# Delta-rule recurrences feeding an MLP mixer: a stretch of the hand-written issue order is rewritten

## Chip, cores and metric

One Trainium2 chip, one of its cores. The metric is device microseconds (us) of one execution of the whole program; several executions are timed and their median is given. One further execution is recorded by the hardware profiler; its times are used for everything that is said about single instructions.

## What is computed

Two blocks follow each other. The first is a delta-rule attention over 4 batch elements, 8 heads, 768 positions and head size 48; the second is an MLP-mixer over its output (768 positions x 384 channels for each batch element). Everything is float32.

```python
k_n = k / (norm(k) + 1e-06)
state = zeros((B, H, D, D))
for t in range(S):
    y[:, :, t] = q[:, :, t] @ state
    v_old = state applied to k_n[:, :, t]
    state += beta[t] * outer(k_n[:, :, t], v[:, :, t] - v_old)
x = y.transpose(0, 2, 1, 3).reshape(B, S, H * D)          # 4 x 768 x 384
xt = x.transpose(0, 2, 1)
h = maximum(xt @ w_tok1, 0) @ w_tok2                      # mixes 768 positions through 256
u = x + h.transpose(0, 2, 1)
out = u + maximum(u @ w_ch1, 0) @ w_ch2                   # mixes 384 channels through 1536
```

## The kernel before

The sequence is cut into chunks of 64 positions, so that one chunk of all 8 heads is handled by small matmuls instead of 64 single steps. Two chunks form a unit of 128 positions. There are 24 units (6 for each batch element) and 48 chunks (12 for each). Units 0 to 5 belong to the first batch element, 6 to 11 to the second, 12 to 17 to the third.

The kernel is written as many small jobs, each a Python generator. Each `next()` on a job issues a handful of instructions, a step, and a long text, `order`, says which job takes its next step when. `p11*4` is four steps of job `p11`. Nothing reorders the result: on each engine, and on the DMA queue that SP issues, instructions run in exactly the order in which the steps stand, each engine at its own pace and held up only by its own waits. This text is therefore a schedule for six queues at once. A step is written here as job and count: r9.5 is the fifth step of r9. The jobs, with their lines:

- `k`u loads keys and queries of unit u (lines 360 to 413); `v`u loads values (413) and scales them on POOL (423, 426).
- `p`u prepares a unit: norms, a masked scale on POOL (511), and turned keys and queries, by PE transposes (499, 519) with ACT copies (503, 524) in units below 12 and by DVE transposes (369) later.
- `c`u and `d`u are the products of keys with keys and queries (PE, 452) and their masking (DVE, 455), for the two chunks of a unit.
- `t`u, `i`round, `f`u invert the triangular 32 x 32 blocks of a unit. Rounds 0 to 6 take several units each; round 2 is units 6 to 9, round 3 is units 10 to 13. A round is 30 pairs of DVE operations, each pair dependent on the one before (676 and 681: i2.2 to i2.31 in round 2), between a DMA in (670) and a DMA out (700); `t` (623) and `f` (648) carry the blocks to and from device memory.
- `h`u and `j`u join inverted blocks into 64 x 64 ones: a DVE transpose (750), 32 x 32 matmuls (780, 783, 788, 821, 829), and ACT copies out of PSUM (799, 802, 806, 755, 834). A wide join has its products at eight places in two PSUM banks.
- `r`t is one chunk's recurrence, a chain through three engines: r.1 to r.4 the product of keys and state (PE, 857, tile `p_k`), r.5 `rest` = that less the values (DVE, 864), r.6 `p_y` and `p_w` (PE, 877 and 881; it needs the unit joined, that is, the last copies of `j`), r.7 the copy `w_t` (ACT, 887), r.8 `p_s` and `p_y` (PE, 895 and 896), r.9 the new state (DVE, 904), r.10 the output (ACT, 909), which also frees the PSUM of `p_y`. The first chunk of a batch element has no r.1 to r.4 of this kind and one step less after them. The tiles `p_k`, `p_y`, `p_w`, `p_s` share two PSUM buffers.
- `m`b is the mixer of batch element b: m.1 to m.6 the first product (PE, 1055), one step for each unit, which needs both chunks of that unit; then the second product (1068), transposes (1078), the channel product (1135 for the first batch element, 1027 later) and the last product (1157), with adds and combinations on DVE (1072, 1086, 1109).
- `w`n loads and rounds a piece of the weights: DMA (271), two ACT operations (277, 278), one DVE operation (280), one POOL operation (284), for some also DVE differences (299); `s` builds sums of weights on DVE (966, 968).
- `z` is one 128 x 128 by 128 x 512 matmul on zeros (225), `Y` four 64 x 64 by 64 x 128 matmuls on zeros (235). They compute nothing that is used. Each is two rows in the profile for each matmul, as is every float32 matmul here.

The DMA queue, the ACT queue and the DVE queue each carry recurrence steps and preparation steps mixed. The part of the text that the change rewrites is at lines 1249 to 1275.

Of the kernel before, what the change touches and what calls it, by code (L numbers as in the profile page):

```python
# [23 lines left out]
def kernel(  # L24
# [1232 lines left out]
    f9*2 w32 f9 j9 f9 r13*2 f8 m0 r13 t10 r13 w31 w32 c11 w32*2 d11*2 c11 v8 c11*3  # L1257
    d11 r14*2 d11*2 r14*3 v8*2 w31*2 r13 w31 k13*5 w30 p12*3 m0*3 r14 c12 d12 c12
    d12 c12 d12 r14 d12 k13*2 r14*3 m0 k13 d12 w30*3 c12*2 v8*2 p13*3 r15*3 k13*4
    r15 t11*3 t12*2 r15 m0*2 r15*2 p13*2 w29 p13 w25 p13 m0*5 r15*2 w33*2 p11 c13*2  # L1260
    d13*2 c13*2 d13 r16*2 k14 c13 d13*2 w33*3 k14*2 r16*2 m0*2 w23 w33 w31*2 w23
# [13 lines left out]
    s*2 m0 i4 m0*2 i4*2 m0 i4*5 v12*4 m0*2 j13 i4*2 m0 i4 r23 j13 m0 r24 k18*3  # L1275
    r24*3 j13 v13*2 r24 i4 r24*2 p18 i4 p18 m0 i4 p18 m0*2 i4*2 m0 r25*3 p18 r25
    p18*2 r25 m1*3 k18*2 v14 i4 v14 r24 i4*7 k19 m1*3 i4 r25 i4*2 k19*3 v13 k19*2
    v14*2 m1 r25 v13 i4*4 k19 m1 p18 m1 k19 r25*2 p18 m1*2 r26 v13 d18 r26*4 j13
    r25 m1*3 r26*2 c18*2 m1*2 r26*2 k19*4 p19*2 d18*3 c18*2 d18 f14*2 v14 r27*2
    f14*2 r27 p19*2 r27 p19 j14 r27 m1*4 s m1*2 f15*3 m1*2 c18 r26 m1*2 r27*2 j14  # L1280
    j15 j14 r27 f16 m1*3 j15*2 r27 r28*2 k20 p19*2 f16 r27 r28*2 k20*2 f16 j16 m1*4
    r28*3 f15 m1*2 s k20*2 s p19 r28 k20*3 d19 c19 k20 d19 p20 c19 t18 k20 d19*2
    p20 c19 v15 r28 p20 r29 k20*2 m1 p20 r28 c19 r29*3 v15*3 f17*2 r29 m1 p20 k21
    m1*2 c19 k21 r29*2 m1*2 d19 k21 m1*2 p20 m1*2 p20 m1*4 r29*3 m1*2 j16*2 r30
    k21*3 v16 k21*2 v15 k21 r30*4 v16 k21*2 m1 k21 m1*2 c20 r30 d20 c20*3 p21*2 c20
    r30*2 p20 d20 r30 d20*2 p21*2 d20 r31*2 r30 r31*2 t18 r31*3 p21*3 m1*2 r31*2
    c21 d21 c21 d21 c21 d21 v16 m1 v16 c21 v16 r32 d21 r32 d21 m1 t18*2 m1 r32 r31
    t19*2 r32*2 f17 m1 f17 m1*4 t19*2 c21 m1*5 p21 m1*2 f16 t20*3 j17*2 t20 t21*4
# [56 lines left out]
```

## Time and profile before

| what | value |
|---|---|
| time, median of 3 | 639.58 us (638.39 to 640.07) |
| the profiled execution's own time | 637.11 us |
| its span, first to last instruction | 635.3 us |
| PE (matmul) busy | 607.5 us, 96% |
| DVE busy | 446.2 us, 70% |
| ACT busy | 268.5 us, 42% |
| POOL busy | 108.2 us, 17% |
| mean granted TensorE clock | 0.981 |

A busy PE is not a PE at its peak: matmuls overlap, and a matmul's row is longer than the distance to the next one. In the views of single instructions the columns are start, duration (or the stretch that a merged row covers), engine, source line, operation, output and inputs, and in brackets the engine's idle time before it and what ended it. In the views of stretches, each engine's busy time is followed by its number of instructions, then come the granted clock (1.00 is full), the busy share of the DMA engines and their rate.

### The profile page before, as it was taken

The numbers are of one execution on the slowest core, as the hardware profiler recorded it, in microseconds if no ns is written. First come the engines' busy times: TensorE is split into PE (matmuls) and PEld (weight loads), VectorE is DVE, ScalarE is ACT, GpSimd is POOL, SyncE is SP. The second block draws the span as 40 slices with busy tenths as digits, with TensorE's granted clock in tenths as the row PEclk, the third lists the DMA queues.
The fourth block names the chain that finished last, engine by engine and source line by source line (L and its number), as shares of the span: only waits on it lengthen the run. The fifth ranks groups of instructions, "written<-read, shape, count | busy, mean of one in ns | idle before, by whom it ended". The sixth has DMA issues, their size and how long they took to land.

```text
span 635.3 us, 21547 instructions
## 1 busy us (share of the span) xinstructions
PE 607.5 (96%) x9132; PEld 529.5 (83%) x9132; DVE 446.2 (70%) x1132; ACT 268.5 (42%) x693; POOL 108.2 (17%) x146
## 2 busy tenths in 40 slices
PE   8488898999999999999999999999999999999997
PEld 5367786667888888858999999769999977999997
DVE  4988877977899667987969987785627253373643
ACT  7759785447512342226624433145254230223240
POOL 2338354235310221111110010101010000000000
PEclk9979896999999999999999999999999999999999
DMA  9787566666542445154444033201020000000000
GB/s 201 129 148 166 140 134 162 170 135 157 110 115 74 82 118 110 50 125 77 95 101 103 14 95 47 66 11 37 2 54 2 27 1 0 26 1 26 2 26 26
DMA packets 135776, 50.27 MB, mean 79 GB/s; under 512 B 114656, under 2 KB 130144, under 8 KB 135680
## 3 DMA queue, kind: packets, MB, share of 16 engines
q1 hardware_dynamic: 135680, 48.89, 34.9%
q8 instruction: 72, 1.18, 0.8%
q14 instruction: 24, 0.20, 0.1%
HBM read 39.42 MB, written 9.44 MB: 77 GB/s over the span
## 4 chain that ended last, share of the span: by engine, by line
PE 78%; DVE 7%; ACT 5%; SPq 3%; DMA 3%; issue 2%; POOL 1%; ACTq 0%; POOLq 0%; DVEq 0%
PE p_o L1157 25%; PE p_r L1027 18%; PE p_c L1135 8%; PE p_h L1068 5%; PE p L1055 4%; PE p_s L895 3%; PE p_g L452 3%; PE p_k L857 3%; PE p_y L877 2%; DVE x L681 1%; DVE sub L676 1%; PE p_w L881 1%; SPq L413 1%; PE p_ut L1078 1%; DMA d<-in_moe_w_ch_dram 1%
## 5 line engine op out<-in xcount | busy, mean ns | idle before, releaser
L1157 PE MATMUL p_o<-wc,r 128*128 128x192 f32 x720 | 126.8, 330 | 0.6 <-ACT u_t L1082 0.6
L1157 PEld LDWEIGHTS p_o<-wc,r 128*128 128x128 f32 x720 | 116.6, 190 | 2.9 <-ACT u_t L1082 1.1
L1039 DVE TENSOR_TENSOR r<-r,p_r 128x512 f32<-128x512 f32 x90 | 59.7, 684 | 39.7 <-PE p_r L1027 37.2
L1086 DVE TENSOR_TENSOR xb<-xb,p_o 128x192 f32<-128x192 f32 x84 | 29.3, 350 | 58.7 <-PE p_o L1157 58.4
L1036 ACT COPY r<-p_r 128x512 f32<-128x512 f32 x54 | 31.5, 586 | 89.4 <-PE p_r L1027 88.0
L681 DVE TENSOR_TENSOR x<-x,sub 128x84 f32<-128x84 f32 (+24 forms) x178 | 59.8, 336 | 6.1
L676 DVE TENSOR_TENSOR sub<-x 128x84 f32<-128x84 f32 (+24 forms) x178 | 57.4, 322 | 6.7 <-DMA x<-n_dram 2.3
L1135 PE MATMUL p_c<-u_t,wc 128*128 128x256 f32 x216 | 51.1, 387 | 0.2 <-ACT u_t L1082 0.2
L1157 PE MATMUL p_o<-wc,s 128*128 128x192 f32 x288 | 50.1, 329 | 0.3 <-DVE xb L1086 0.3
L426 POOL TENSOR_TENSOR v_st<-v_st,nrm 128x384 f32<-128x384 f32 x24 | 20.3, 845 | 166.7 <-DMA v_st<-in_v_dram 129.1
L1157 PEld LDWEIGHTS p_o<-wc,s 128*128 128x128 f32 x288 | 46.8, 190 | 1.2 <-DVE xb L1086 0.6
L1135 PEld LDWEIGHTS p_c<-u_t,wc 128*128 128x128 f32 x216 | 39.6, 190 | 6.1 <-ACT u_t L1082 0.4
L1043 ACT ACTIVATE r<-r 128x512 f32<-128x512 f32 x54 | 33.8, 630 | 25.0 <-DVE r L1039 24.6
L452 PE MATMUL p_g<-kq 48*64 48x128 f32 (+1 forms) x704 | 38.6, 283 | 3.0 <-ACT kq L524 2.8
L511 POOL TENSOR_TENSOR mb<-mask_c,cs 128x512 f32<-128x512 f32 x20 | 21.4, 1072 | 108.0 <-DVE cs L489 40.9
L909 ACT ACTIVATE xb<-p_y 64x192 f32<-64x192 f32 x96 | 31.2, 325 | 19.6 <-PE p_y L896 12.1
L1027 PE MATMUL p_r<-u_t,wc 128*128 128x128 f32 x288 | 38.5, 277 | 0.0
L1027 PE MATMUL p_r<-t_d,wc 128*128 128x128 f32 x288 | 37.2, 280 | 0.0
L887 ACT COPY w_t<-p_w 128x192 f32<-128x192 f32 x48 | 15.3, 318 | 50.0 <-PE p_w L881 49.3
L1027 PEld LDWEIGHTS p_r<-u_t,wc 128*128 128x128 f32 x288 | 35.3, 192 | 0.3
L1055 PE MATMUL p<-xb,w 128*128 128x384 f32 x96 | 34.9, 511 | 0.0
L452 PEld LDWEIGHTS p_g<-kq 48*64 48x64 f32 (+1 forms) x704 | 28.9, 137 | 7.1 <-ACT kq L524 3.7
(184 smaller groups left out, 1216.0 us busy)
## 6 DMA issues: line engine op xcount, KB each, us to landing
d<-in_moe_w_ch_dram SPq DMA_DIRECT2D x24, 384.0 KB, 4.2
v_st<-in_v_dram SPq DMA_DIRECT2D x96, 48.0 KB, 2.7
out_dram<-xb SPq DMA_DIRECT2D x23, 192.0 KB, 1.9
kst<-in_k_dram SPq DMA_DIRECT2D x64, 48.0 KB, 2.8
n_dram<-gm SPq DMA_DIRECT2D x72, 32.0 KB, 2.0
pads<-in_k_dram SPq DMA_DIRECT2D x24, 96.0 KB, 3.1
pads<-in_q_dram SPq DMA_DIRECT2D x24, 96.0 KB, 2.5
gm<-w_dram SPq DMA_DIRECT2D x72, 32.0 KB, 2.1
```

The source lines that it names most:

```text
L452: nc.tensor.matmul(p_g[PAR[i ^ cc], p], kqt[f, p, cc, 0], kqt[f, p, cc])
L676: nc.vector.tensor_tensor(out=tmp, in0=y[:, :, 0:s, s : s + 1].to_broadcast([n, k, s, w]), in1=y[:, :, s : s + 1, s + 1 : m].to_broadcast( ...
L681: nc.vector.tensor_tensor(out=y[:, :, 0:s, s + 1 : m], in0=y[:, :, 0:s, s + 1 : m], in1=tmp, op=ALU.add,)
L909: nc.scalar.mul(y[:, :, D * i : D * i + D], p_y[PAR[1 - i]], 1.0 if c else -1.0)
L1027: nc.tensor.matmul(p[:, i], pieces[i // width][:, at : at + 128], f[f"u{n}"], start=first and i == 0, stop=True, skip_group_check=True,)
L1036: nc.scalar.copy(o, p)
L1039: nc.vector.tensor_tensor(out=o, in0=o, in1=p, op=ALU.add if sign > 0 else ALU.subtract)
L1043: nc.scalar.activation(o, o, ACTF.Relu)
L1055: nc.tensor.matmul(p_1[dh], piece_of(w1, c, 0)[:, dh * 128 : (dh + 1) * 128], xb[:, c], start=(c == 0), stop=(c == NCH - 1),)
L1068: nc.tensor.matmul(p_h, piece_of(w2, j, c * 128)[:, c * 128 : (c + 1) * 128], r1[j], start=(j == 0), stop=(j == NDH - 1),)
L1135: nc.tensor.matmul(p_c[:, k], piece_of(wc1, cb, f * 128)[:, f * 128 : (f + 1) * 128], u_t[:, cb], start=(cb == 0), stop=(cb == NCB - 1),)
L1157: nc.tensor.matmul(p, a[:, m], wc2[:, m, j], start=(start and i == 0), stop=(i == NM - 1), skip_group_check=True,)
```

## The change

Only the text `order` changes. The steps up to k11.2 and h5.6, just after r8.9, stand as before, and so do those from the loads of unit 18 and round 4 on (k18, i4, r24), apart from weight sums and one step of f12; between them, over the recurrences r9 to r23, the second and third inversion rounds, the units' preparation and most of the first mixer block, the same steps stand in another order. Jobs take the same steps; only the matmuls on zeros differ in number: two `z` are added and two of three `Y` in the stretch are gone. The functions and the PSUM layout are unchanged, the joins' eight places in two banks among them.

The first lines of the diff, which carry the recurrences r9 to r13:

```diff
-    w29 w27*2 r8*2 w29*3 j4*2 r8 w22*4 t9*4 r8*3 p10 h5*2 k11 h5 j5 Y i2 r9*3 r8
-    r9*2 i2*4 j5 i2*3 r9*2 i2 h5 k12*2 j5 Y r9*2 m0 v6 k11 j5 p9 w4*2 r10*3 i2*2 j5
-    k10 r10 p10*4 w4 v5 i2 v5*3 r9 k11*2 v5 r10*3 i2 w4 i2*3 w15*3 w19*2 i2 w19 m0
-    i2 w12 r10*2 m0*2 r11 r10 p11 k12*4 w19 p11 p10 k12*2 p12 Y i2 w25 r11*3 d10*4
-    r11*2 v7 c10*3 w15 k12 i2*2 w21 i2*4 v6*3 r11*2 i2*3 k11 r11 v7*4 i2*4 c10
-    k12*3 m0*4 c10 m0*2 w25 m0 w12 d10 f6*4 f7*2 p11*2 m0*3 w12 w21 w12 p12 p11*2
-    m0*2 f7 w21*2 j6*2 j7 v6 p12 w25*3 f8*2 w27*2 m0 j6 j7*2 m0 r12*5 f8 f7 j8*2
-    r12 m0 w23*4 j8 r12 t10 r12 t10*2 r13 p10 w23 r13*4 w20*2 p11*3 p12*2 w20*2
...
+    w29 w27*2 r8*2 w29*3 j4*2 r8 w22*4 t9*4 r8*3 p10 h5*2 k11 h5 p9 h5 m0 w4*3 i2
+    j5 i2*3 r9*4 z r8 r9 k11*2 p10*2 i2*4 p10 i2 j5*2 r9*4 m0 r10 k10 p10*2 w21 w4
+    w21 v5*2 i2*2 z i2*2 r10 d10 r10*2 j5 r9 i2 m0 v5 d10 v5*2 w19*2 r10 j5 r10
+    c10*2 i2*3 k12 w19 k12*5 w15*3 k12 w19 r10*3 v7*3 r10 c10*2 r11*2 d10*2 r11 i2
+    r11 m0 r11 w15 r11 k11*2 p11 i2*9 w25 i2*3 v6 r11*2 v6*3 r11 m0*3 k12 v7 k12*2
+    i2 w12*2 i2 m0*2 c10 d10 t10 m0*5 w12*2 t10 p11 w25 p11*4 v6 w25 p12*3 w21 m0*3
+    p10 f6*3 j6*3 w21 w23*2 w25 f7*3 m0 f7 f6 j7*2 m0 f8*3 j7 r12*2 w27*2 f9 r12 j8
+    r12 v7 r12*2 w23*3 w32*2 t10*2 r12*2 k12 w32*2 j8*2 r13*5 Y p12*2 p11*2 w25
...
```

Further on, in the same manner, the third inversion round (i3), the preparation of units 10 to 17 and the recurrences r13 to r23 are dealt differently among the steps of the mixer; four of the weight sums, which stood among r18 to r23, come together after them:

```diff
-    i3 v10*3 m0*7 p15 m0*3 r18*2 m0 f10*4 m0*3 r18 s f12*2 v10 r18 s p14 s m0 r18
...
-    c15*2 r21 v11 r21 r20 f13 r21*2 d15 f13*2 p16 m0*2 v11 p16 r21*2 j12*2 p16*2
-    r21*3 k17*3 m0 p15 t14*2 j13 r22*2 d16 r22*3 m0 r22 s c16 d16*2 c16 d16*2 r22
-    k17*9 t14 t15 r22 m0 r22 r23 c16 v12 r23 c16 r23 s c16 t16 r23 t15*2 r22 p17
-    t15 p16 r23 m0 r23 p17 t16 p17*5 m0*4 f13 t16*2 r23*2 d17 t14 c17 d17 c17 d17
-    c17 d17*2 c17*2 t17*4 k18*2 i4 k18 s*4 m0 s k18 m0 k18*3 m0 p17 m0 s f12 m0*4
...
+    r21*2 j12*2 p16*4 k17*4 r21*2 p16 m0 d16 r22*2 d16 r22*2 p15 r21 k17*7 v11 m0
+    r22 k17 r22*2 f13 f12 c16 d16*3 c16 s j13 c16 r22 t15 m0 r22 r23 v12 r23 c16
+    r23 c16 t16 r23 t15*2 r22 p17 t15 r23 m0 r23 p17 t16 p17*5 m0*4 t16*2 r23*2 d17
+    t14*4 c17 d17 c17 d17 c17 d17*2 c17*2 t17*4 k18*2 i4 k18 s*8 m0 s k18 m0 k18*3
+    m0 p17 m0 s m0*4 s*2 m0 i4 m0*2 i4*2 m0 i4*5 v12*4 m0*2 j13 i4*2 m0 i4 r23 j13
```

More of the change, by code (lines that the diff above doesn't have):

```diff
@@ L1255 @@
-    m0*2 f7 w21*2 j6*2 j7 v6 p12 w25*3 f8*2 w27*2 m0 j6 j7*2 m0 r12*5 f8 f7 j8*2
-    r12 m0 w23*4 j8 r12 t10 r12 t10*2 r13 p10 w23 r13*4 w20*2 p11*3 p12*2 w20*2
[L1257 to L1261, printed above, removed]
@@ L1275 @@
[L1275 to L1281, printed above, removed]
@@ L1282 @@
[L1282 to L1288, printed above, removed]
@@ new lines @@
+    r12 v7 r12*2 w23*3 w32*2 t10*2 r12*2 k12 w32*2 j8*2 r13*5 Y p12*2 p11*2 w25
+    p11*2 w31*2 f9*2 r13*2 m0 r13 w31*2 f8 f9 r13 j9 c11*2 w23 d11 w20*2 k12 w30
+    c11 d11 v8 c11*2 d11 w20*2 r14*2 d11 r13 r14 d11 r14*2 p12*2 v8*2 m0*3 w30*2
+    p12 r14 m0 r14*3 w30 d12 k13*4 d12 k13*8 c12 r14 c12 d12 c12 w29 d12*2 p13*2
+    c12 w27 c12 w25 r15*5 m0*2 p13*4 m0 r15 p13 r15 m0*4 t11*2 r15 p13 c13*2 d13
+    w25 c13 r15 c13*2 t11 d13 r16 d13 r16 r15 t11 d13 v8 t12*2 w33 v8 d13 w33*5
+    r16*3 w29 m0 t12*2 m0 w33 j9 m0*2 w31 k14 w31 k14*6 j9 t13*2 r16*2 t13*2 j9 w23
@@ new lines @@
+    k14 r16*3 i3 p14*3 m0 v9 r17*5 v9 w31 p14 k14*2 p14*2 k15*2 j9 m0*2 v10*3 i3*3
+    r17 i3*4 m0*3 r17 i3 k14*2 m0 v9*2 r17*3 i3*2 m0*2 i3*2 v10 m0*3 k15*3 p14 c14
+    p14 d14 c14 d14 r18 d14 r18*2 d14 k15*3 p15 i3 k15 i3 r18 i3*9 m0*2 i3*8 k15*3
+    m0*2 v9 r18 m0*2 f10*3 p15 f12 m0*9 f11*4 r18*2 m0 r18*3 f10 m0 d14 c14 f12*2
+    r19*2 c14*2 r19*3 m0*3 j10 p15*3 k16*3 p15 v10 f13 r19 p15 j10 j11 r19*2 k16*2
+    j10 k16*2 m0*2 k16*3 j11 r19 r20*2 r19 r20*3 m0 j11 r20 m0 r20 v11*3 k16 v11
@@ new lines @@
+    k16 r20*3 d15 c15 d15 c15 d15 c15*3 d15 r21*2 d15 j12 r21*3 m0*2 f13*2 p16*3 m0
+    r21*2 j12*2 p16*4 k17*4 r21*2 p16 m0 d16 r22*2 d16 r22*2 p15 r21 k17*7 v11 m0
[3 more added lines that the diff above has]
+    m0 p17 m0 s m0*4 s*2 m0 i4 m0*2 i4*2 m0 i4*5 v12*4 m0*2 j13 i4*2 m0 i4 r23 j13
@@ new lines @@
+    m0 r24 k18*3 r24*3 j13 v13*2 r24 i4 r24*2 p18 i4 p18 m0 i4 p18 m0*2 i4*2 m0
+    r25*3 p18 r25 p18*2 r25 m1*3 k18*2 v14 i4 v14 r24 i4*7 k19 m1*3 i4 r25 i4*2
+    k19*3 v13 k19*2 v14*2 m1 r25 v13 i4*4 k19 m1 p18 m1 k19 r25*2 p18 m1*2 r26 v13
+    d18 r26*4 j13 r25 m1*3 r26*2 c18*2 m1*2 r26*2 k19*4 p19*2 d18*3 c18*2 d18 f14*2
+    v14 r27*2 f14*2 r27 p19*2 r27 p19 j14 r27 m1*4 s m1*2 f15*3 m1*2 c18 r26 m1*2
+    r27*2 j14 j15 j14 r27 f16 m1*3 j15*2 r27 r28*2 k20 p19*2 f16 r27 r28*2 k20*2
+    f16 j16 m1*4 r28*3 f15 m1*2 s k20*2 s p19 r28 k20*3 d19 c19 k20 d19 p20 c19 t18
@@ new lines @@
+    k20 d19*2 p20 c19 v15 r28 p20 r29 k20*2 m1 p20 r28 c19 r29*3 v15*3 f17*2 r29 m1
+    p20 k21 m1*2 c19 k21 r29*2 m1*2 d19 k21 m1*2 p20 m1*2 p20 m1*4 r29*3 m1*2 j16*2
+    r30 k21*3 v16 k21*2 v15 k21 r30*4 v16 k21*2 m1 k21 m1*2 c20 r30 d20 c20*3 p21*2
+    c20 r30*2 p20 d20 r30 d20*2 p21*2 d20 r31*2 r30 r31*2 t18 r31*3 p21*3 m1*2
+    r31*2 c21 d21 c21 d21 c21 d21 v16 m1 v16 c21 v16 r32 d21 r32 d21 m1 t18*2 m1
+    r32 r31 t19*2 r32*2 f17 m1 f17 m1*4 t19*2 c21 m1*5 p21 m1*2 f16 t20*3 j17*2 t20
@@ new lines @@
+    t21*4 k22 i5 k22*5 j17 k22 m1*2 k22 i5*3 r32 k22 i5*2 m1 i5 m1 r32*3 i5 k22
+    m1*4 p22*2 i5 v17 p22 r33*2 k22 r33*3 p22 m1*4 p22 m1 k23 p22 i5 v20 i5*3 m1*2
+    r32 m1*4 k23 i5 k22 r33 p22 r33 v17 j17 m1*4 r33 i5 m1*6 k23 r33 k23 m1*6 k23
+    m1*2 j17 v20 m1 v17*2 k23*2 m1*6 r34*2 d22 v17 k23 r34*3 m1*6 r33 i5*4 m1 r34
+    p23*2 c22 d22 c22 d22 c22 d22 i5*2 r34*2 m1 r34 m1 i5*4 m1*4 v20*2 p23 r35*2
+    k23*3 c22*2 r35 k23 i5*3 r35 m1*4 i5*3 m1*6 p23 m1*4 d22 t22 r34 i5 m1 p23*2
+    m1*4 t22*2 r35*2 m1 f20 p23 m1 r35 m1*2 p23 f21*2 v20 f18 m1*2 v18 m1*3 t22
@@ new lines @@
+    m1*2 f18*3 d23 c23 d23 v18 c23 d23 m1 v18 f19*4 c23 d23 m1 c23*2 f20 r35*2 m1*5
+    d23 t23*4 m1*2 j18*3 j19 f20 v18 m1 j19 m1*2 j20 i6*2 m1*4 i6*2 v18 j19 r36*5
+    j20 r36 i6*2 m2 r36 r37 i6*2 r36 r37*3 m2*3 r37*2 m2 i6*8 v19*2 r37*3 m2 r38
+    r37 v19 f20 v19 i6*4 f21 j21 r38 v19 r38*3 m2*3 j20 r38*2 i6*2 j21 r38*2 i6*4
+    m2*3 f21 r39 r38 r39*4 m2*7 v21*2 r39*2 m2*4 j21 m2*5 r39*3 m2*2 r40*4 m2 r40*2
+    j21 i6*2 r40*2 v21 j21 m2*2 i6 v21 m2*2 i6*3 f22*3 r40*2 r41*5 f22 m2*4 r41*2
@@ L1308 @@
+    m2*7 r41*3 m2 v21 m2*2 r42*2 j22 r42 f23 r42 j22 r42*3 m2*5 f23*2 m2*8 r42*2
+    j23 m2*13 p22 m2 v22*3 j22 v22 m2*3 r43 m2 r43*2 r42 r43*2 m2 r43*2 m2*6 r43 m2
+    j23 v23 r43*2 r44*4 v22 j23 r44 m2 v23*2 m2*3 r44*2 m2 r44 m2*5 r44 m2*3 r44
+    m2*3 v23 r45*5 m2*8 r45 m2*2 r45 f23 j23*2 m2*2 r45*3 m2*6 r46*4 m2*2 v23 r46
+    m2*9 r46*2 m2*2 r46*3 m2*7 r47*5 m2*6 r47 m2 r47 m2*2 r47 m2*6 r47 m3*6 m2*5
+    m3*6 m2*11 m3*3 m2 m3*159
     """
```

26 lines of the change are left out of this document (removed).

## The prediction

> **What bounds the kernel now.** I read the page first (busy shares, slices, chain), then stretches along the span, then the waits of PE, then single instructions where the order changes.
>
> ```profile
> span 635.3 us, 21547 instructions
> ...
> PE 607.5 (96%) x9132; PEld 529.5 (83%) x9132; DVE 446.2 (70%) x1132; ACT 268.5 (42%) x693; POOL 108.2 (17%) x146
> ...
> PEclk9979896999999999999999999999999999999999
> ...
> PE 78%; DVE 7%; ACT 5%; SPq 3%; DMA 3%; issue 2%; POOL 1%; ACTq 0%; POOLq 0%; DVEq 0%
> ```
>
> PE leads the chain of work, and every slice with a reduced clock lies in the first fifth. By stretches (PE busy comes first after the length):
>
> ```profile
> 122.00:140.00 18.00, 17.81 (x155) 11.81 (x152) 13.81 (x41) 7.22 (x19) 3.85 (x5) 1.00 0.59 135
> 140.00:180.00 40.00, 39.57 (x831) 33.79 (x830) 31.18 (x74) 24.43 (x72) 16.51 (x18) 1.00 0.58 135
> 180.00:240.00 60.00, 59.95 (x992) 52.36 (x992) 46.21 (x120) 19.07 (x55) 8.11 (x11) 1.00 0.42 95
> ```
>
> From 122 us to 240 us PE is idle 0.19 + 0.43 + 0.05 = 0.67 us. The rewritten part runs from 103 us to about 244 us, so nearly all of it lies where PE is full. Another order there cannot save what PE does not waste; it can only save the little that PE waits, or lose more. What can be saved lies ahead of 122 us, where PE waits for one recurrence after another and its clock is halved:
>
> ```profile
> PE p_s L895 <- ACT w_t L887: 1.0, 1, 1.0
> PE p_y L877 <- ACT xb L909: 0.9, 1, 0.9
> PE p_w L881 <- ACT gm L755: 0.9, 1, 0.9
> ```
>
> ```profile
> 97.99:101.41 3.42, 2.06 (x70) 1.52 (x66) 1.42 (x6) 2.94 (x9) 2.02 (x2) 1.00 0.61 152
> 101.41:104.82 3.41, 2.66 (x58) 2.57 (x60) 1.30 (x5) 1.99 (x7) 2.55 (x3) 0.50 0.57 182
> 104.82:108.23 3.41, 3.41 (x102) 3.33 (x104) 3.02 (x12) 1.20 (x4) 0.44 (x2) 0.50 0.87 195
> 108.23:111.65 3.42, 3.42 (x27) 1.65 (x24) 3.15 (x11) 0.86 (x3) 0.36 (x1) 0.50 0.47 78
> ```
>
> The first view is of PE's waits from 96 to 124 us, the second of stretches of 3.41 us, at whose borders the clock switches here. So the yardstick is one moment: when r11.8 is issued, after which m0.5, m0.6 and the rest of mixer block 0 keep PE full. Now that is:
>
> ```profile
> 47.55 1.12 PE L225 MATMUL p_warm<-warm 128*128 128x512 f32 x2
> ...
> 103.05 1.09 PE L235 MATMUL p_warm<-warm 64*64 64x128 f32 x8
> ...
> 108.48 2.93 PE L1055 MATMUL p<-xb,w 128*128 128x384 f32 x4
> ...
> 111.34 0.80 PE L829 MATMUL p_x<-gm,zst 32*32 32x32 f32 x32
> ...
> 112.07 0.67 PE L857 MATMUL p_k<-s_t,kq 48*64 48x48 f32 x16
> ...
> 113.16 0.60 PE L519 MATMUL p_t<-ident,lent 128*128 128x128 f32 x4
> ...
> 117.38 2.85 PE L1055 MATMUL p<-xb,w 128*128 128x384 f32 x8
> ...
> 124.02 0.59 PE L1055 MATMUL p<-xb,w 128*128 128x384 f32 x1
> ```
>
> m0.5 begins at 124.02 us. What sets it is DVE, whose queue the third inversion (round 2) fills between the steps of r9 to r11:
>
> ```profile
> 110.06 0.35 DVE L904 TENSOR_TENSOR s_t<-s_t,p_s 128x192 f32<-128x192 f32 x1
> ...
> 113.69 0.34 DVE L864 TENSOR_TENSOR rest<-p_k,v_st 128x192 f32<-128x192 f32 x1
> ...
> 119.06 1.10 DVE L681 TENSOR_TENSOR x<-x,sub 128x238 f32<-128x238 f32 x1
> ...
> 120.09 0.34 DVE L904 TENSOR_TENSOR s_t<-s_t,p_s 128x192 f32<-128x192 f32 x1
> 120.35 0.54 DVE L479 TENSOR_REDUCE ksum<-ksq 128x8 f32<-128x384 f32 x1
> 120.81 0.48 DVE L676 TENSOR_TENSOR sub<-x 128x234 f32<-128x234 f32 x1
> ...
> 121.65 0.35 DVE L864 TENSOR_TENSOR rest<-p_k,v_st 128x192 f32<-128x192 f32 x1
> ```
>
> ```profile
> 103.32:121.65 18.33, 17.07 (x300) 12.50 (x298) 16.77 (x48) 8.85 (x23) 5.68 (x8) 0.77 0.69 169
> ```
>
> The two L864 rows are r10.5 and r11.5, the two L904 rows r9.9 and r10.9; from r8.9 to r11.5 DVE (third figure after the length) is busy for 16.77 of 18.33 us. PE began m0.3 at 117.38, right behind r10.8, so r10's new state could have been formed soon after that; it was formed at 120.09, since i2.17, i2.18 and two weight pieces stand ahead of it.
>
> **The change, part by part.** *(A) r9 to r11.* All that stood ahead of r11.5 on DVE still does, but for p11.2 and i2.19, which now stand behind it. From the start of one row to the next they took 120.81 - 120.35 = 0.46 and 121.65 - 120.81 = 0.84 us. By DVE's queue alone r11.5 moves from 121.65 to 120.35. But r10.5 now stands behind i2.14 and no longer behind i2.12, so the recurrence might be late at another place. I walk it.
>
> m0.1 takes the place of the first Y, at 103.05, still at half clock: its four instructions take 111.34 - 108.48 = 2.86 us there, against 2.85/2 = 1.4 at full clock. Of the three half-clock stretches above only the last, filled with these dense 128 x 384 matmuls, was followed by the full clock; the one before it, as busy but with small tiles, was not. I take the clock to return at 104.82, more than half of the stretch before being m0.1 then. So m0.1 is issued by 103.05 + 1.77 + (1 - 1.77/2.86) x 1.4 = 105.35 and r9.4 (0.67, the row at 112.07) by 106.0. The matmul z behind it (at most 1.12) fills PE while DVE answers. Ahead of r9.9 DVE has the rows it has now and w4.3 besides, so r9.9 stays at about 110. From there ACT decides:
>
> ```profile
> 112.19 0.74 ACT L755 COPY gm<-p_x 32x256 f32<-32x256 f32 x2 [3.07 <-PE p_x L829]
> ...
> 113.96 0.66 ACT L909 ACTIVATE xb<-p_y 64x192 f32<-64x192 f32 x2
> ...
> 115.48 0.32 ACT L887 COPY w_t<-p_w 128x192 f32<-128x192 f32 x1 [0.86 <-PE p_w L881]
> ...
> 115.69 0.56 ACT L277 ACTIVATE d<-d 128x384 f32<-128x384 f32 x1
> 116.14 0.55 ACT L278 ACTIVATE d<-d 128x384 uint32<-128x384 uint32 x1
> ...
> 118.60 0.56 ACT L524 COPY kq<-p_t 128x512 f32<-128x512 f32 x1
> ```
>
> PE issues m0.2 (1.4) from 110, r10.1 and p10.8 (0.6) by 112.0; 0.2 later p10.8's result is there. ACT must then do p10.9 (0.56), w21.2 (1.1), r9.10 (0.66), w19.2 (1.1) and j5.5 (0.74), 4.2 us, before r10.6 may start, at 116.4. DVE is no later: 110.4 + five pairs of i2 at 0.84 + 0.34 = 114.95 for r10.5, and 1 us more if POOL stretches two pairs like the 1.10 row. p_w runs 0.9; w15.2 (1.1) holds ACT until 117.5, w_t until 117.8, r10.8 ends at 118.75 and r10.9 at 119.1, against 120.43 now. r11.1 to r11.4 are issued by 119.7; i2.18 (0.84, or 0.7 more if stretched) ends between 119.95 and 120.65, and r11.5 starts at about 120.3. DVE's queue alone gave the same 1.3 us. But m0.4 now stands between r11.4 and r11.6: 119.7 + 1.4 = 121.1 instead of 121.65 + 0.3. So 0.85 us are left at r11.6, and 0.3 more because the last products of unit 10, which stand between r11.8 and m0.5 now, are done earlier: **m0.5 at about 122.85, 1.2 us earlier**, with the same useful matmuls behind it. Bounds: with the clock back only at 108.23, m0.1 and z take their double length and all moves 1.2 us, a gain of 0; if DVE is spared a third of its 1.56 us of idle time as well, 1.8. I take 1.2, where both queues agree.
>
> *(B) Matmuls on zeros.* The two z and the lost Y lie where PE waits anyway and cost nothing beyond (A); without that cover two z would cost twice 1.12. The Y that is left stands behind r13.4 now, where PE is full: eight instructions, 1.09 us at half clock by the row at 103.05, so at most 0.55 at full clock and 0 if r13.5 is awaited there. I take 0.3.
>
> *(C) r12.* Between r12.4 and r12.6 stood j8.2, which filled PE while ACT copied w_t; now nothing stands there.
>
> ```profile
> 143.37 0.90 PE L881 MATMUL p_w<-v_st,gm 64*64 64x48 f32 x16
> ...
> 145.36 0.25 PE L895 MATMUL p_s<-w_t,gm 64*64 64x48 f32 x1
> ```
>
> The stretch is 1.99 us with about 1.0 of j8.2's work in it; bare it is 0.9 + 0.32 + two hand-overs of 0.1 = 1.4, so 0.4 is lost, less what j8.2, now in front of r13, waits less for its banks. I take 0.2 (0 to 0.4).
>
> *(D) Four weight sums* (s.2 to s.5) go behind r23 in front of s.6.
>
> ```profile
> 247.43 1.41 DVE L968 TENSOR_TENSOR wc<-wc 128x512 f32<-128x512 f32 x2
> ...
> 251.03 0.56 DVE L1109 TENSOR_TENSOR s<-r 128x384 f32<-128x384 f32 x1 [2.19 <-ACT r L1144]
> ```
>
> Four times 0.7 is 2.8 us; DVE idles 2.19 us behind s.11, which hides all but 0.6. A mixer add is then 0.6 late, but each pair of adds has two PSUM banks and PE is a whole product (about 1.1) behind. Cost 0; if the banks don't cover it, 0.6.
>
> *(E) Everything else from r13 to r23* is the same work in other places on full queues, 0.67 us of PE waits to win and as much or more to lose: 0, bounds -0.7 and +1.5 (three waits of the first view, 1.0 each at most, half of them covered).
>
> Sum against the profiled execution: 637.11 - 1.2 + 0.3 + 0.2 = 636.4 us. It lies 2.47 us below the median of the runs shown, so for the median I forecast 639.58 - 0.7 = **638.9 us**.
>
> The Trainium skill speaks to the clock here. In the rows, the stretch from 97.99 has PE busy for 2.06 of 3.42 us and no wait over 1.0, and half clock follows; the one from 104.82 is busy throughout, and half clock stays. "TensorE: Matmul & The Clock Gate", section "What's actually happening", has the clock drop after at least one idle window of about 3.4 us and return after one busy window. By that rule the drop at 101.41 would not be there, nor could one come from waits of 1 us in the new order, and the gain would be (A)'s by the queues alone, 638.9 again, with no chance for the slower rival below. The trace contradicts the rule on both counts, so the rival stays.
>
> **The rivals.** *Faster:* the new order also takes away waits of PE behind 122 us. For it: they exist (0.67 us between stretches, 0.4 within j8.2), (A) reaches its 1.8, and (B) and (C) vanish in answers awaited anyway. Then -1.8 - 0.67 - 0.4 = -2.9: 636.7 us. Against it: ACT's 4.2 us ahead of r10.6 leave little slack.
>
> *Slower:* the clock drops a second time, around r10.6 to r11.6. Its place: between 116 and 121 us PE waits for ACT ahead of r10.6, for w_t ahead of r10.8 and for DVE ahead of r11.1, with little but 64 x 48 matmuls between, much as from 97.99 on. Against it: m0.3 and m0.4, dense, lie close. Its price: behind it stand dense m0 steps, so that each 3.41 us at half clock costs 1.7 us; one stretch gives -0.7 + 1.7 = +1.0, 640.6 us, still no change; from two on it decides: -0.7 + 3.4 = +2.7, 642.3 us, and three, as now, 644.
>
> **How the numbers follow.** A measurement of this kernel tells a difference of about 0.3%, 1.9 us, from none. The forecast with its bounds (gain 1.8 and B, C at 0: 637.8; gain 0, B and C at 0.95: 640.5) lies within that: chance 0.44. One further stretch at half clock: 0.04, also within. Faster rival: 0.28, and 0.01 for more than it. Slower rival with two stretches or more, or (E) at its worst with (D): 0.23. So faster 0.29, within 0.48, slower 0.23. The likeliest case's own range is 637.8 to 640.5; the range goes to the slower rival, 642.3, and on the fast side 1.2 us past the faster one (as far as the lowest run shown lies below the median), 635.5.
>
> **What would show it.** Right: full clock again from about 105 us, m0.5 near 122.9, r10.6 released by ACT's j5.5 copy, r10.9 no longer late, PE idle below 1 us from 123 to 244. Wrong: half clock at 117 or later (slower rival); m0.5 at 124 or later with the clock back only at 108 (no gain); new waits of PE over 0.5 us behind 125, above all at r12.6, at the joins of units 6 to 9 or at the adds around 250; or m0.5 as said and the end earlier by far more, which would be work that I have put down as equal.

## The result and the profile after

| | kernel before | changed kernel |
|---|---|---|
| median of 4 executions each, run side by side | 638.99 us (638.35 to 640.07) | 642.77 us (642.35 to 643.15) |
| the profiled execution's own time | 637.11 us | 642.35 us |

The ratio is 1.0054 with a 95% interval of 1.0033 to 1.0075: slower by about 3.8 us, and outside the forecast range. A second comparison (the first kernel of the second set below) gave 1.0038 (1.0015 to 1.0061).

The page of the changed kernel:

```profile
span 640.3 us, 21521 instructions
...
PE 611.0 (95%) x9120; PEld 530.4 (83%) x9120; DVE 445.8 (70%) x1132; ACT 268.6 (42%) x693; POOL 107.0 (17%) x146
...
PEclk9979797998999999999999999999999999999999
...
PE 79%; DVE 7%; ACT 5%; DMA 3%; issue 2%; SPq 2%; POOL 1%; ACTq 0%; POOLq 0%; DVEq 0%
```

The shares hardly move: the span grew by 5.0 us, PE's busy time by 3.5 us with 12 matmul records fewer. The slices are 16 us long and too coarse to show where. The waits of PE show it, first from 96 to 127 us, then from 127 to 250 us (total, times, longest):

```profile
PE p_s L895 <- ACT w_t L887: 2.2, 3, 1.3
PE p_w L881 <- ACT gm L755: 0.8, 1, 0.8
```

```profile
PE p_t L519 <- ACT gm L802: 1.7, 1, 1.7
PE p_s L895 <- ACT w_t L887: 0.4, 1, 0.4
PE p_w L881 <- issue: 0.3, 1, 0.3
```

The wait of 1.7 us in the stretch where PE was full before is new. Stretches at the places where the clock switches (length, PE busy, PEld, DVE, ACT, POOL, granted clock, DMA share, GB/s) show that a second thing is new there:

```profile
98.36:101.77 3.41, 2.13 (x73) 1.67 (x69) 1.77 (x5) 2.60 (x9) 2.06 (x3) 1.00 0.60 147
101.77:105.19 3.42, 2.51 (x35) 1.81 (x36) 0.99 (x4) 2.05 (x8) 2.40 (x3) 0.50 0.89 243
105.19:108.60 3.41, 3.41 (x20) 1.74 (x19) 2.85 (x11) 1.12 (x4) 1.32 (x3) 0.50 0.90 226
108.60:112.01 3.41, 2.84 (x102) 2.21 (x100) 3.13 (x9) 1.63 (x4) 0.83 (x1) 1.00 0.86 210
...
146.18:149.59 3.41, 2.99 (x136) 2.45 (x135) 1.31 (x4) 2.51 (x8) 0.76 (x2) 1.00 0.90 215
149.59:153.00 3.41, 1.74 (x39) 1.47 (x39) 2.47 (x6) 3.10 (x12) 2.33 (x3) 1.00 0.78 205
153.00:156.42 3.42, 3.42 (x51) 2.59 (x53) 0.80 (x3) 2.12 (x5) 1.00 (x1) 0.50 0.80 203
125.19:240.00 114.81, 112.08 (x1853) 93.63 (x1849) 84.98 (x220) 48.42 (x139) 27.61 (x34) 0.99 0.47 109
```

The clock came back at 108.60 us, not at 104.82; and it fell once more at 153.00 us, behind a stretch in which PE was busy for 1.74 of 3.41 us. The Trainium skill, "TensorE: Matmul & The Clock Gate", section "What's actually happening", has the drop come after at least one idle window of about 3.4 us; this stretch was half busy, so the trace again disagrees.

The last row is the middle of the program, from the start of m0.5 to that of r23.1. The same stretch of the kernel before:

```profile
124.02:235.34 111.32, 110.65 (x1838) 92.20 (x1836) 87.35 (x222) 48.75 (x140) 28.38 (x33) 1.00 0.50 114
```

So I cut the time in four: up to r8.8 (the same steps in both kernels, 102.16 and 102.68 us), the **head** from r8.8 to m0.5 (21.9 and 22.5), the **middle** (111.3 and 114.8), and the rest (635.3 - 235.34 = 400.0 and 640.3 - 240.00 = 400.3). Of 5.0 us, the middle has 3.5. In single instructions (the queue of ACT, then two rows of PE):

```profile
147.92 0.56 ACT L277 ACTIVATE d<-d 128x384 f32<-128x384 f32 x1 [0.62 <-DMA d<-in_moe_w_ch_dram]
148.37 0.55 ACT L278 ACTIVATE d<-d 128x384 uint32<-128x384 uint32 x1
148.94 0.66 ACT L909 ACTIVATE xb<-p_y 64x192 f32<-64x192 f32 x2
149.62 1.06 ACT L799 COPY zst<-p_z 32x128 f32<-32x128 f32 x4
150.69 1.07 ACT L802 COPY gm<-p_z 32x128 f32<-32x128 f32 x4
```

```profile
151.26 0.66 PE L519 MATMUL p_t<-ident,lent 128*128 128x128 f32 x4 [1.69 <-ACT gm L802]
...
152.46 2.43 PE L1135 MATMUL p_c<-u_t,wc 128*128 128x256 f32 x6
```

The two rows of copies are j8.3, which empties the two banks of the join of unit 8. p11.8, the transposes of unit 11, takes the first of these banks, which the second of the four L802 copies empties, and r13.6 stands behind p11.8 on PE. That copy by itself:

```profile
150.96 0.26 ACT L802 COPY gm<-p_z 32x128 f32<-32x128 f32 x1
```

It ended at 151.21 us, and the transposes began 0.05 us later. (So it is in all five profiles with a wait at p11.8.) j8.3 is late because it stands behind the weight piece w32.2, which waited for its DMA, and r12.8, and because its products, j8.2, now run from 147.96 us and no longer from 144.20. Then the clock falls, and m0.20 takes 2.43 us. Against the kernel before, r13.1 starts 1.18 us later (as m0.5 did, 1.17), r13.6 3.11 us and m0.22 4.70 us later: 1.9 us for the wait, 1.6 for the half clock, and the difference stays there (4.66 at r23.1). In the kernel before the same place had little to spare:

```profile
145.86 1.06 ACT L799 COPY zst<-p_z 32x128 f32<-32x128 f32 x4
146.94 1.07 ACT L802 COPY gm<-p_z 32x128 f32<-32x128 f32 x4
```

```profile
147.21 0.26 ACT L802 COPY gm<-p_z 32x128 f32<-32x128 f32 x1
```

```profile
148.06 0.66 PE L519 MATMUL p_t<-ident,lent 128*128 128x128 f32 x4
```

The copy that empties p11.8's bank, the second of L802, ended at 147.47 us. The transposes began 0.6 us later, without a wait, behind r13.4. Against the start of r13.1 the change moved the end of that copy by 2.6 us (from 0.0 to 2.57 us behind it) and left the transposes where they were: 2.6 less 0.6 is about the 1.9 us that were lost.

### The profile page after: what moved, and what is told of

Its sections match the earlier page's. It is cut to its first block, busy times and chain, and to the rows that moved or that the text cites. A ratio compares the mean times of both kernels' runs of the same rounds, so it can differ in the third digit from the quotient of the medians.

```text
span 640.3 us, 21521 instructions
## 1 busy us (share of the span) xinstructions
PE 611.0 (95%) x9120; PEld 530.4 (83%) x9120; DVE 445.8 (70%) x1132; ACT 268.6 (42%) x693; POOL 107.0 (17%) x146
## 4 chain that ended last, share of the span: by engine, by line
PE 79%; DVE 7%; ACT 5%; DMA 3%; issue 2%; SPq 2%; POOL 1%; ACTq 0%; POOLq 0%; DVEq 0%
PE p_o L1157 24%; PE p_r L1027 18%; PE p_c L1135 7%; PE p L1055 5%; PE p_h L1068 5%; PE p_g L452 3%; PE p_s L895 3%; PE p_k L857 3%; PE p_y L877 3%; PE p_w L881 1%; DVE x L681 1%; DVE sub L676 1%; PE p_ut L1078 1%; PE p_y L896 1%; SPq L413 1%
## 5 line engine op out<-in xcount | busy, mean ns | idle before, releaser
L1027 PEld LDWEIGHTS p_r<-t_d,wc 128*128 128x128 f32 x288 | 33.9, 192 | 0.9
```

The source lines that it names most:

```text
L1027: nc.tensor.matmul(p[:, i], pieces[i // width][:, at : at + 128], f[f"u{n}"], start=first and i == 0, stop=True, skip_group_check=True,)
```

## The experiments

Theory: the loss is made at r12 and r13, by the wait at p11.8 for the joins' banks and by the clock that falls because r12's small matmuls stand bare. Rival: it is made by r9 to r11, or by the steps moved from r14 to r23. All kernels compute the same; only `order` differs. In the first set the kernel before had a median of 637.85 us, in the second 638.45, then 640.21, 639.56 and 640.44; each ratio goes with its own set.

**Half of the change each.** The changed order up to r11.9 and then the remaining steps in the order of before; and the reverse.

```diff
 (e1)  changed order up to r11.9 | order of before, the steps that are left
 (e2)  order of before up to r11.9 | changed order, the steps that are left
```

> The order of the change up to r11.9, then the remaining steps in the order of before. Theory (the loss comes behind r12, where PE waits at p11.8 for the two PSUM banks that j8.2 holds, and half clock follows): m0.5 about 0.7 us later than in before at most, no wait over 0.5 us at p11.8, no half clock after 112 us, time within 0.15% of before. Rival (the loss comes from r9 to r11, the wait at p11.8 is only its echo): 0.4% or more slower, like the change.

> The order of before up to r11.9, then the remaining steps in the order of the change. Theory: the wait at p11.8 (1.5 to 2 us) and a stretch of half clock behind it are there although r9 to r11 run as before; 0.4% to 0.6% slower than before. Rival (r9 to r11 are to blame): within 0.15% of before.

Measured: 644.67 us, ratio 1.0104 (1.0073 to 1.0136), and 642.75 us, 1.0068 (1.0039 to 1.0096). At the seams ACT stands still ahead of m0.7: in e1 behind p12.1, which waits until 132.57 us for a reduction that stands behind the inversion on DVE, in e2 behind a weight piece that waits 2.7 us for its DMA. PE's waits, of e1 and then of e2:

```profile
PE p_h L1068 <- ACT r L1063: 5.7, 1, 5.7
```

```profile
PE p_h L1068 <- ACT r L1063: 1.8, 1, 1.8
...
PE p_t L519 <- ACT gm L802: 1.2, 1, 1.2
```

The waits at m0.7 belong to the seams, and behind e1's the clock fell (130.5 to 137.4 us), so these times decide nothing on halves. The profiles say more. From r12.1 to r23.1, in the order of before, e1 takes 91.8 us and the kernel before 92.0: the changed r9 to r11 ahead of them cost them nothing. e2 shows that the wait at p11.8 comes with the later steps; its clock held behind it.

**p11 later; more cover.** e3 moves p11.8 to p11.10 behind m0.20. e4 puts two matmuls on zeros ahead of p11.8.

```diff
 (e3)
-p12*2 p11*2 w25 p11*2 w31*2 f9*2 r13*2 m0 r13
+p12*2 p11 w25 w31*2 f9*2 r13*2 m0 p11*3 r13
 (e4)
-p12*2 p11*2 w25
+p12*2 p11 z*2 p11 w25
```

> The change, with only p11.8 to p11.10 (the second transposes of unit 11, their copy and the last scale) moved from in front of r13.6 to behind m0.20. Theory: PE does r13.6 and m0.20 while ACT empties the banks, the 1.7 us wait goes, and with it the half clock behind it: 3.5 us less than the change, about 639.3 us, within 0.15% of before. Rival (the wait only moves to r13.6 or c11, because ACT and the joins are late as a whole): at most 1 us less than the change, 641.8 us or more.

> The change, with two more z (matmuls on zeros, 1.1 us together with four instructions of 512 columns at full clock, 1.7 at most) directly in front of p11.8. The wait stays, but PE is busy in it. Theory (the half clock at 153 us follows from the idle wait): full clock from 109 us to the end, 1.6 us less than the change, about 641.2 us, 0.3% over before. Rival (the clock drops for another reason, or the matmuls on zeros only push the rest back): half clock stays, 642.8 us or more.

Measured: 640.88 us, ratio 1.0041 (1.0019 to 1.0062), and 640.41 us, 1.0043 (1.0024 to 1.0061). The stretches at r12 and r13, of e3, then of e4:

```profile
144.47:147.88 3.41, 2.53 (x114) 1.93 (x112) 0.98 (x3) 3.08 (x10) 0.77 (x2) 1.00 0.89 237
147.88:151.30 3.42, 3.42 (x80) 2.85 (x59) 2.18 (x6) 3.07 (x11) 2.75 (x3) 0.50 0.85 196
```

```profile
144.24:147.65 3.41, 2.70 (x122) 2.20 (x122) 1.13 (x5) 2.90 (x9) 1.48 (x2) 1.00 0.82 207
147.65:151.07 3.42, 3.42 (x44) 2.21 (x43) 2.42 (x5) 2.38 (x7) 1.32 (x2) 1.00 0.82 245
```

In e3 the wait at p11.8 is gone, and the clock falls all the same, earlier and for two stretches (r13.6 to m0.22 take 6.95 us instead of 4.06, p11.8 now among them). In e4 the zero products lie where PE waited: no wait is left at p11.8, and the clock holds, although r12 is as bare there as in e3. r13.6 comes as late behind r13.1 as in the changed kernel (1.9 us more than before), but this is not the price of the wait alone: p11.8's bank was free at 148.18 us, and the last 0.9 of the 1.8 us that the two z took (1.1 to 1.7 expected) ran after that. So the clock can fall without this wait, and neither edit took away both losses.

In the changed kernel itself the drop came behind the stretch with the wait, not behind the one with most of r12 (from 146.18 us). That the bare r12 drops the clock there, as the theory has it, is not shown. Nor is it shown that filling the wait holds it: without the z, e4's wait would have been about 0.9 us (147.3 to 148.2), and those of 1.1 and 1.2 us (e8, e2) were not followed by a drop.

**The changed kernel again, three repairs, and one move alone.** e6 puts j8.2 and j8.3 back around r12.6. e7 has e3's move and one z on each side of r12.1 to r12.4. e8 is the kernel before with one edit: j8.2 and j8.3 behind r12.8.

```diff
 (e6)
-r12 v7 r12*2 w23*3 w32*2 t10*2 r12*2 k12 w32*2 j8*2 r13*5
+r12 v7 r12 j8 r12 j8 w23*3 w32*2 t10*2 r12*2 k12 w32*2 r13*5
 (e7, with e3's)
-f8*3 j7 r12*2 w27*2 f9 r12 j8 r12 v7 r12*2
+f8*3 j7 z r12*2 w27*2 f9 r12 j8 r12 z v7 r12*2
 (e8, in the order of before)
-r12*5 f8 f7 j8*2 r12 m0 w23*4 j8 r12 t10 r12 t10*2 r13
+r12*5 f8 f7 j8 r12 m0 w23*4 r12 t10 r12 j8*2 t10*2 r13
```

> The change itself once more, so that the next three stand beside it on one chip. Both theories: 0.5% to 0.75% slower than before; the wait at p11.8 (1.5 to 2 us) is there in the profile, the half clock near r12 and r13 in most executions, so in the profile with a chance of about 2 in 3.

> The change, with only j8.2 moved back in front of r12.6 and j8.3 right behind r12.6, as they stood in before. Theory (j8 behind r12.8 costs twice: the banks come free late, and r12 stands bare, so that the clock drops): the wait at p11.8 under 0.5 us, no half clock between 125 and 160 us, 2.5 to 3.5 us less than the change in the same call, within 0.2% of before. Rival (the loss is spread over the new order, or lies in r9 to r11): less than 1 us better than the change.

> The change, with p11.8 to p11.10 behind m0.20 as in the earlier run, and one more z each in front of r12.1 and behind r12.4. Theory (two separate costs, the wait for the banks of about 1.9 us and the half clock after the bare r12 of 1.6 to 3.3 us): neither is left, at 0.4 to 0.9 us for the two z; 2.5 to 3.5 us less than the change, 1 to 2 us less than with p11 moved alone. Rival (the half clock comes from elsewhere): half clock near 150 us stays, and the time is that of p11 moved alone or above.

> The kernel before, with only j8.2 and j8.3 moved behind r12.8, where the change has them. Theory: this one move makes most of the loss: p11.8 waits 1 to 2 us for the banks, half clock follows in part of the executions, 0.2% to 0.5% slower than before. Rival: PE is full there and the same work only changes places, 0 to 0.1% slower.

Measured: e5 642.02 us, ratio 1.0038 (1.0015 to 1.0061); e6 642.09, 1.0058 (1.0038 to 1.0079); e7 639.43, 1.0025 (1.0002 to 1.0049); e8 641.15, 1.0033 (1.0007 to 1.0059). PE's waits behind 127 us in e5, then in e8:

```profile
PE p_t L519 <- ACT gm L802: 2.6, 1, 2.6
```

```profile
PE p_t L519 <- ACT gm L802: 1.1, 1, 1.1
```

e5 repeats both signs (half clock from 153.15 to 156.56 us, middle 115.7 us). e8 makes the wait out of the kernel before with the one move, as the theory has it; its clock holds in r13 (the theory had the drop in part of the executions), its middle is 112.7 us, and no more than about 1 us of its loss can be put down to that wait. e6 missed: it lost the wait at p11.8, but r12.6 stopped for 1.0 us without a releaser in the profile, and the clock fell from 149.14 to 152.55 us. e7 has neither sign; its middle, and the two stretches at r12:

```profile
123.63:236.65 113.02, 112.26 (x1856) 92.95 (x1852) 85.54 (x221) 48.41 (x139) 27.44 (x34) 1.00 0.47 111
144.18:147.59 3.41, 3.41 (x59) 1.76 (x58) 0.37 (x2) 2.50 (x8) 0.89 (x1) 1.00 0.89 241
147.59:151.01 3.42, 3.23 (x129) 2.79 (x126) 2.64 (x6) 3.13 (x11) 2.57 (x3) 1.00 0.85 214
```

Its middle is 1.8 us shorter than the changed kernel's although two z of about 1 us each have been added. In the medians this is 2.6 us against e5, as expected, but the intervals of the two ratios overlap.

**Real work for cover; the head.** e9 surrounds r12 as in the kernel before (j7.2 ahead of m0.18, j8.2 behind r12.5, m0.19 and j8.3 behind r12.6, w32.2 behind r12.8). e10 moves m0.1 behind r9.4, e11 does both. e12 is the kernel before with one z ahead of r8.6 and one behind it.

```diff
 (e9)
-j6*3 w21 w23*2 w25 f7*3 m0 f7 f6 j7*2 m0 f8*3 j7 r12*2
+j6*3 f7*4 f6 j7*3 w21 w23*2 w25 m0 f8*3 r12*2
...
-r12 v7 r12*2 w23*3 w32*2 t10*2 r12*2 k12 w32*2 j8*2 r13*5
+r12 v7 r12 j8 r12 m0 j8 w23*3 w32 t10*2 r12*2 w32*3 k12 r13*5
 (e10)
-p9 h5 m0 w4*3 i2 j5 i2*3 r9*4 z r8 r9
+p9 h5 w4*3 i2 j5 i2*3 r9*4 m0 z r8 r9
 (e12, in the order of before)
-j4*2 r8 w22*4
+j4*2 z r8 z w22*4
```

> The changed order, with the surroundings of r12 as in the kernel before: the two z products of unit 7 (j7.2) and their copies ahead of m0.18, j8.2 between r12.4 and r12.6, m0.19 and then j8.3 behind r12.6, w32.2 behind r12.8. All else stays changed. Theory (the loss behind 125 us is made in r12 and r13 alone): PE no longer waits over 0.5 us at p11.8, no half clock between 140 and 165 us, r13.6 and m0.22 no later against m0.15 than in the kernel before (within 0.5 us); what is left of the loss is that of r9 to r11, so the ratio to before is 1.000 to 1.002, about 638.5 to 640. Rival (the loss comes from work moved elsewhere, r14 to r23): the half clock goes but the ratio stays at 1.004 or above.

> The changed order with one step moved: m0.1 stands behind r9.4 and no longer ahead of r9.1. Theory (r9 to r11 gained nothing because r9.1 to r9.4 queue behind m0.1, 2.9 us at half clock, so that r9.5 and with it the DVE pairs and r9.9 come 1.6 us later against r8.8 than before): r9.5 comes within 3.5 us of r8.8 (5.2 to 5.7 in the changed order), r9.9 within 8.5 us (9.5), m0.5 within 21.5 us (22.5), and the r12 loss stays, so the ratio is 1.002 to 1.004. Rival (ACT's copies ahead of r10.6 set it all): r9.9 is earlier but m0.5 still stands at 22.2 us or more behind r8.8.

> Both of the two kernels just named in one: r12 surrounded as before, and m0.1 behind r9.4. Theory: the gains add, PE waits less than 1 us between 125 and 240 us, m0.5 within 21.5 us of r8.8: 637 to 638.5 us, ratio 0.997 to 1.000. Rival (each of them only moves the wait): no better than the better of the two alone.

> The kernel before with two matmul pairs on zeros more, one ahead of r8.6 and one behind it, where PE waits for ACT's copies. Theory (the clock drops at 101.4 us because PE does little in the 3.41 us ahead, and half clock there costs nearly nothing, since DVE's inversion pairs set r9 to r11): no half clock between 95 and 115 us, or one stretch of 3.4 us at most, and m0.5 less than 1 us earlier against r8.6 than in the kernel before; ratio 0.998 to 1.001. Rival (the half clock of 10.2 us is what r9 to r11 lose): m0.5 earlier by 2 us or more, ratio 0.996 or below.

Measured: e9 643.40 us, ratio 1.0054 (1.0033 to 1.0075); e10 643.68, 1.0060 (1.0033 to 1.0087); e11 641.74, 1.0021 (0.9996 to 1.0045); e12 640.72, 1.0005 (0.9990 to 1.0020). e9's profile did as the theory says of wait and clock, but two other waits came in, 0.9 us for w_t and 0.6 us for the transposition ahead of j8.2. Behind m0.15, r13.6 and m0.22 come 1.3 and 1.9 us later than in the kernel before, where at most 0.5 was expected; the middle is 113.3 us, and the median did not fall. e11 missed too: head 23.0 us, middle 113.4, no gains to add. e10's theory failed, and its middle is the longest of the order as changed, 117.3 us, with a wait of 2.0 us at p11.8 and half clock from 154.3 to 161.1 us. DVE's queue there:

```profile
106.50 0.44 DVE L750 STREAM_TRANSPOSE t<-gm 128x256 f32<-128x256 f32 x1
109.29 0.19 DVE L676 TENSOR_TENSOR sub<-x 128x30 f32<-128x30 f32 x1 [2.35 <-DMA x<-n_dram]
...
110.69 0.35 DVE L864 TENSOR_TENSOR rest<-p_k,v_st 128x192 f32<-128x192 f32 x1
```

The last row is r9.5. Its products were there early, but the change has put i2.2 to i2.4 ahead of it, and these wait 2.35 us for the DMA that brings the blocks of the round. In the changed kernel that wait was 0.2 us, hidden by m0.1, and 1.9 in e4. e12 has no half clock from 95 to 115 us; r10.6 comes 11.4 us behind r8.8 instead of 12.5, but the clock falls from 115.5 to 122.4 us instead, and the kernel gains nothing. What the half clock of the head alone costs stays open.

**Useful products between r12.4 and r12.6, and the kernel before against itself.** e13 moves m0.19 behind r12.4 and has e3's move. e14 adds to it w19.3, w15.3 and w19.4 behind r10.9, d10.3 and d10.4 behind r11.6, i2.18 behind r11.5.

```diff
 (e13, with e3's)
-j7*2 m0 f8*3 j7 r12*2 w27*2 f9 r12 j8 r12 v7 r12*2
+j7*2 f8*3 j7 r12*2 w27*2 f9 r12 j8 r12 m0 v7 r12*2
 (e14, with e13's)
-k12 w19 k12*5 w15*3 k12 w19 r10*3 v7*3 r10 c10*2 r11*2 d10*2 r11 i2 r11 m0 r11 w15 r11 k11*2
+k12*6 w15*2 k12 r10*3 w19 w15 w19 v7*3 r10 c10*2 r11*4 m0 r11 i2 w15 r11 d10*2 k11*2
```

> The changed order with m0.19 moved behind r12.4, so that dense useful products lie where ACT copies w_t, and p11.8 to p11.10 moved behind m0.20; nothing is added. Theory (the loss behind 125 us is the wait at p11.8 and the half clock that the bare r12 brings): no half clock from 140 to 165 us, no wait over 0.5 us at p11.8, r13.6 and m0.22 at least 2.5 us earlier against m0.5 than in the changed order (whose m0.22 lies 32.3 us behind m0.5), ratio to before 1.000 to 1.002. Rival (moved work costs as much elsewhere, or j8 waits in turn): m0.22 no more than 1.5 us earlier against m0.5, ratio 1.003 or above.

> The kernel just named, with four small moves in r10 and r11 besides: the pieces w19.3, w15.3 and w19.4 behind r10.9, the products d10.3 and d10.4 behind r11.6, and i2.18 behind r11.5. Theory (at full clock the forecast's r10.9 came 0.5 us late behind the two weight pieces, and m0.4 0.9 us late behind d10.3, d10.4 and the rest): r10.9 starts within 0.1 us of r10.8's end, m0.5 0.3 to 1.2 us earlier against r8.8 than in the kernel just named, ratio lower by 0.0005 to 0.002. Rival (ACT's copies ahead of r10.6 set it, and the moved products only come later): m0.5 within 0.3 us of the kernel just named.

> The kernel before, unchanged. Ratio 1.000 within 0.002. Theory (half-clock stretches end and begin on a grid whose phase differs from run to run): its profile has other half-clock stretches than the first one, above all around 100 to 122 us, and differs by 1 to 3 us from it between r8.8 and m0.5 or ahead of r8.8; it has no half clock and no wait over 0.5 us from 125 to 250 us. Rival (the stretches belong to the order): they lie where they lay, within 1 us.

Measured: e13 642.74 us, ratio 1.0036 (1.0018 to 1.0053); e14 641.73, 1.0038 (1.0024 to 1.0052); e15 639.22, 0.9998 (0.9977 to 1.0019). e13 missed. PE's longest wait behind 127 us there:

```profile
PE p_w L881 <- issue: 1.8, 1, 1.8
```

It lies at r12.1, which now comes right behind j7.2 and starts at 144.81 us, in the middle of ACT's copies j7.3 (143.33 to 145.53 us). I read it as r12.1 waiting for these copies, though the profile names no releaser. m0.19 had covered this: moved to one gap, it opened another, and the clock fell at 145.4 us. e14 has the same wait and one of 1.2 us for DVE ahead of a second product (L1068); its clock holds, and its middle is 114.5 us all the same. e14's head is 0.4 us shorter than e13's (22.1 and 22.5 us), at the low end of what was expected; the ratio shows nothing of it. The profile of e15:

```profile
111.49:114.91 3.42, 2.41 (x54) 1.96 (x53) 3.31 (x8) 1.96 (x5) 1.59 (x2) 0.99 0.85 248
114.91:118.32 3.41, 3.41 (x33) 1.71 (x23) 3.18 (x9) 2.09 (x5) 0.00 (x0) 0.51 0.81 202
...
125.05:237.06 112.01, 110.89 (x1838) 92.56 (x1837) 87.54 (x222) 48.67 (x140) 28.22 (x33) 1.00 0.50 113
```

The unchanged kernel has a second drop in its head in this execution, near the place where the prediction put it for the changed one, and a head of 23.5 us instead of 21.9. Its middle has full clock again. It did wait 0.8 us once behind 125 us, which the theory had excluded.

**e9 again, and one z alone.** e16 is e9 once more, for its profile; e17 is e7 without the z ahead of r12.1.

> The kernel with r12 surrounded as before, once more. If its first profile was typical: a middle (m0.5 to r23.1) of 113 to 114 us and no half clock between 125 and 240 us. If it was one of the better executions: a middle of 115 us or more, with a half-clock stretch in r12 or r13, since 0.6 and 0.9 us of waiting stand close together there.

> The changed order with p11.8 to p11.10 behind m0.20 and one z behind r12.4. Theory (what matters is that the stretch of small matmuls at r12 is broken by a dense product): no half clock between 140 and 165 us, a middle (m0.5 to r23.1) of 112 to 113.2 us, ratio to before 0.999 to 1.003. Rival (one z is too little): a half-clock stretch there, a middle of 114.5 us or more, ratio 1.003 to 1.005.

Measured: e16 (one execution, 642.29 us) has a middle of 113.9 us with full clock, so e9's first profile was typical, and part of the median of that kernel stays unexplained. e17 takes 640.83 us, ratio 1.0013 (0.9992 to 1.0034), full clock in r12 and r13, middle 113.8 us: between what theory and rival gave.

All profiles by head and middle (starts of r8.8, m0.5 and r23.1):

| order of the part | heads, us | middles, us |
|---|---|---|
| as before | 21.9, 22.9 (e8), 23.5 (e15) | 111.3, 111.1 (e12), 112.0 (e15) |
| as changed | 22.5, 22.6 (e5), and 22.1 to 23.0 in e3, e4, e6, e7, e9, e13, e16, e17 | 114.8, 115.7 (e5), 117.3 (e10) |
| changed, neither of the two | | 113.0 (e7, two z), 113.8 (e17, one z), 113.3, 113.9 and 113.4 (e9, e16, e11), 114.5 (e14) |
| changed, one of the two losses | | 113.9 (e4: delay, two z), 115.0 (e3: half clock), 114.8 (e6 and e13: half clock) |
| before, j8 late | | 112.7 (e8) |

From m0.22 to r23.1 all profiles, of either order, take 82.4 to 83.0 us (before 82.5, changed 82.5). So the steps moved from r14 to r23 lose nothing. With e1's r12 to r23 above, both halves of the rival fall: in the profiles the loss lies in r12 and r13. The medians show this less well. Ahead of r8.8, where all kernels have the same steps, the profiles differ by 5.6 us (r8.8 starts at 100.0 us in e4, at 105.6 in e8), more than the change costs. Nor do the timed executions show more half clock in all for the changed kernel: its mean granted clock over e5's 12 executions is 0.9805, that of the kernel before 0.9792 over 34. In how many executions the clock falls in r13 is open.

## Why the prediction was wrong

The step that failed is **(E)**: everything else from r13 to r23 as the same work in other places, 0 us with an upper bound of +1.5. Between the two profiles the middle lost 3.5 us, 1.9 by the wait at p11.8 and 1.6 by a half-clock stretch; in e5 it was 2.9 and 1.6. Middles of 114.8 to 117.3 us in the changed order stand against 111.1 to 112.0 in that of before, and the medians differ by 3.8 us. The wait could be worked out from the rows of before: p11.8 had 0.6 us to spare, and the order moved the copy that empties its bank behind w32.2, r12.8 and the later j8.2. The bound of (E) came from the size of other waits and not from this queue. The prediction's own signs of being wrong named waits at the joins of units 6 to 9; the wait came at the next user of such a join's bank. The half clock could not be read off those rows. It followed waits of 1.7 to 2.6 us at p11.8 (changed kernel, e10, e5), not those of 1.1 and 1.2 us (e8, e2), and came in e3 without any; the wait of 1.8 us at r12.1 had it behind it in e13 and not in e14. What sets it off is open.

**(C)** had its arithmetic right: r12.1 to r12.6 took 147.35 - 146.04 = 1.31 us, 1.4 forecast. What it left out is that j8.2, moved, gives its two banks back later, to p11.8. The bare r12 next to a hand-over may cost clock as well, as the drop behind it in e3 suggests, but in the changed kernel the clock held behind r12.

**(A)** said -1.2 us; against the one profile of before it was 22.50 - 21.85 = +0.65. Right were the order of the release at r10.6 (it started at 117.98, during ACT's j5.5 copies), r10.9 right behind r10.8, and the two rows that DVE no longer does ahead of r11.5. Wrong were three sizes. The clock came back one stretch later, the forecast's own case of no gain: m0.1 began at 103.72 us instead of 103.05 and filled less than half of the first stretch. At full clock from 103.3 us on (e4) the head was still 22.2 us, since i2.2 waited for its DMA and r9.9 came 9.8 us behind r8.8 instead of 7.8. And from r10.9's start to m0.4's it took 1.4 us instead of about 0.6, with d10.3 and d10.4 between r11.2 and r11.3, which I had not counted. The yardstick was off too: a head of 21.9 us was the shortest of three of before. Over all profiles the heads of the two orders overlap, so (A) neither gained nor lost what can be told.

**(B)** cost nothing where +0.3 was taken: the Y behind r13.4 ended in front of the wait at p11.8. **(D)** was right at 0: from r23.1 to the end the two differ by 0.3 us.

The **slower rival** had the right mechanism, a second clock drop priced at 1.7 us for a stretch (1.6 measured), at the wrong place: there was none from 108.60 to 153.00 us. The **faster rival** fell with (E): PE's waits behind 125 us grew.
